# Pooled attention and a multiplicative feed-forward block in one kernel: when the loads start, when the transposes start, and what GpSimd waits for between them

## The chip, the cores and the metric

One core of one Trainium2 chip. The metric is device time in microseconds (us), lowest is best. Each run is labelled fast or slow. On one core there is no second die to compare, so "slow" here only says that a run took over 1.5% more than the fastest run of the same kernel; comparisons and ratios below use fast runs, and where only slow runs show something, the text says so.

TensorE (PE) does matrix products, VectorE (DVE) and ScalarE (ACT) work element by element, GpSimd (POOL) here only issues loads, and SyncE (SP) issues the DMA transposes and the stores. In the profile, L133 is line 133 of the kernel that was run; the changed kernel's lines are numbered a little differently.

## The reference

Attention over 8 batches, 8 heads, 1152 keys of 64 dimensions, with queries averaged in pairs (576 of them), then a feed-forward block with a product of two branches and no nonlinearity:

```python
q_pool = q.reshape(B, H, S // 2, 2, D).mean(axis=3)
scores = (q_pool @ k.transpose(0, 1, 3, 2)) / sqrt(D)
attn   = softmax(scores)
x      = heads_to_columns(attn @ v)             # 4608 x 512
out    = ((x @ w1) * (x @ w2)) @ w3 @ w_out     # 4608 x 512
```

## The kernel before

Two heads are worked on together; such a **pair** has the number P, from 0 to 31. Keys and queries have to be transposed before the scores. For pairs 0 to 8 TensorE transposes them; from pair 9 (`NPE`) on, DMA does it. Per pair there are three loads (k, q, v, from float32 to float16), a copy `kc` that reorders the keys, the pooling of q, a copy of v, and two DMA transposes:

```python
def load(P):                # a "trio": GpSimd issues k, q and v
    load_k(P); load_q(P); load_v(P)        # kst, vst: 4 buffers; qst: 3, each for two pairs

def new_kq(P):
    kT[P] = ab.tile([128, NJ, 128], FP16, tag="kT", bufs=3, name="kT")
    qT[P] = ab.tile([128, NJ, 64], FP16, tag="qT", bufs=3, name="qT")

def prep_dma(P):
    pp, o = P // 2, 64 * (P % 2)
    new_kq(P)
    kc = ab.tile([128, NJ, 2, D], FP16, tag="kc", bufs=2, name="kc")
    nc.vector.tensor_copy(out=kc.rearrange("p j u d -> p u j d"), in_=kst.pop(P))
    nc.sync.dma_start_transpose(out=kT[P], in_=kc.rearrange("p j u d -> p (j u d)"))
    pool_q(P)
    nc.sync.dma_start_transpose(
        out=qT[P], in_=qps[pp][o:o + 64].rearrange("p c u d -> p (c u d)"))
    copy_v(P)
```

The main loop works in iterations of three 512-wide chunks of scores (`BURST = 3`); `at` is the position of the scores, counted in pairs. Between the scores it puts value matmuls (`pv`) by a fixed plan, and pieces of the feed-forward block:

```python
for it in range(NIT):
    at = it * BURST * CH / PAIR             # 1536 / 5184 = 0.296 pairs an iteration
    for w in range(BURST):
        scores(BURST * it + w)              # TensorE: psc = kT, qT
        expo(BURST * it + w)                # ScalarE: er = exp(psc)
    ...                                     # [cut] pairs below NPE
    while staged >= NPE and loaded < NP and at >= loaded - (5.0 if loaded == 9 else 3.4):
        load(loaded)
        loaded += 1
    ...
    elif prepped < NP and at >= prepped - 1.75:
        prep_dma(prepped)
        prepped += 1
    ...                                     # [cut] value matmuls and feed-forward pieces
```

An output row block is copied by VectorE into `osb` (3 buffers) and stored by SyncE, in the same queue as the transposes:

```python
osbs[i] = ffp.tile([128, dm], FP32, tag="osb", bufs=3, name="osb")
...
nc.vector.tensor_scalar_mul(out=osb, in0=p[:, 0:n], scalar1=1.0 / (SCL * SCL))
...
eng.dma_start(out=dst[f // 64][:, cs], in_=osbs[i][64 * z:64 * z + 64, cs])     # nc.sync
```

The softmax here doesn't subtract the row's maximum and nothing guards it: scores larger than these inputs give would overflow.

## Time and profile before

| | before |
|---|---|
| time, median of the first 3 runs (range) | 457.09 us (451.55 to 460.79) |
| profiled run: time, span | 449.39 us, 447.6 us |
| TensorE busy | 410.6 us, 92% of the span |
| ScalarE, VectorE, GpSimd busy | 73%, 48%, 17% |
| landing of kT, qT (min / median / max) | 3.4 / 7.0 / 22.3 us, 2.8 / 9.4 / 21.5 us |

The page is read from its slices (where is TensorE not full?) to the waits (on what?) to the chain that ended last (is that wait on the path?) to the timelines of single engines. "Landing" is the time from the issue of a DMA until its data are there. The prediction below shows the lines.

### The profile page before, as it was taken

The numbers are of one execution on the slowest core, as the hardware profiler recorded it, in microseconds if no ns is written. First come the engines' busy times: TensorE is split into PE (matmuls) and PEld (weight loads), VectorE is DVE, ScalarE is ACT, GpSimd is POOL, SyncE is SP. The second block draws the span as 40 slices with busy tenths as digits, with TensorE's granted clock in tenths as the row PEclk, the third lists the DMA queues.
The fourth block names the chain that finished last, engine by engine and source line by source line (L and its number), as shares of the span: only waits on it lengthen the run. The fifth ranks groups of instructions, "written<-read, shape, count | busy, mean of one in ns | idle before, by whom it ended". The sixth has DMA issues, their size and how long they took to land.

```text
span 447.6 us, 12693 instructions
## 1 busy us (share of the span) xinstructions
PE 410.6 (92%) x5450; PEld 271.2 (61%) x5450; DVE 214.5 (48%) x445; ACT 327.0 (73%) x356; POOL 74.6 (17%) x113
## 2 busy tenths in 40 slices
PE   3989999991999999974799999999999999999996
PEld 1667787761477567742477567765775686544443
DVE  2556555661454655551354564565555644623130
ACT  4898899882688889873488889889788889323332
POOL 8424233230121121210032021230100000000000
PEclk9999999997899999998799999999999999999999
DMA  8999999999599999999599999999992262031304
GB/s 133 207 208 201 178 199 169 192 186 134 65 159 184 151 140 154 123 135 126 75 162 190 143 135 156 146 178 117 157 171 42 55 103 62 15 72 36 80 16 94
DMA packets 94216, 58.71 MB, mean 131 GB/s; under 512 B 64848, under 2 KB 84560, under 8 KB 94160
## 3 DMA queue, kind: packets, MB, share of 16 engines
q0 software_dynamic: 26544, 33.56, 50.4%
q1 hardware_dynamic: 67456, 24.22, 41.5%
q8 instruction: 42, 0.69, 0.7%
q10 hardware_dynamic: 160, 0.13, 0.1%
q14 instruction: 14, 0.11, 0.1%
HBM read 67.11 MB, written 9.44 MB: 171 GB/s over the span
## 4 chain that ended last, share of the span: by engine, by line
PE 77%; DMA 14%; ACT 6%; issue 1%; DVE 0%; POOL 0%; SPq 0%; ACTq 0%; DVEq 0%; POOLq 0%
PE psc L239 16%; PE po L263 16%; PE pp L374 14%; PE pa L356 13%; PE pb L356 13%; DMA qT<-qp 12%; ACT er L249 6%; PE pT L340 3%; DMA kst<-in_k_dram 1%; PE w3t L328 1%; DMA out_dram<-osb 1%; PE t L153 1%; PE tk L153 0%; POOL qst L79 0%; ACT osb L383 0%
## 5 line engine op out<-in xcount | busy, mean ns | idle before, releaser
L249 ACT ACTIVATE er<-psc 128x1024 f16<-128x1024 f32 x324 | 307.8, 1026 | 69.5 <-PE psc L239 69.2
L263 PEld LDWEIGHTS <-er 128*128 128x128 f16 x2880 | 104.7, 98 | 27.0 <-issue 9.7
L239 PE MATMUL psc<-qT,kT 64*128 64x512 f16 (+7 forms) x1152 | 98.9, 293 | 22.9 <-DMA qT<-qp 17.8
L263 PE MATMUL po<-vt,er 128*128 128x65 f16 x2880 | 112.2, 194 | 3.8 <-issue 3.1
L368 DVE TENSOR_TENSOR gT<-pb,asb 128x512 f16<-128x512 f32 x72 | 49.7, 690 | 63.0 <-PE pb L356 62.4
L239 PEld LDWEIGHTS <-kT 64*128 64x128 f16 x1152 | 46.8, 95 | 48.7 <-issue 17.6
L356 PE MATMUL pb<-xT,w2sb 128*128 128x512 f16 x288 | 75.5, 385 | 0.0
L356 PE MATMUL pa<-xT,w1sb 128*128 128x512 f16 x288 | 75.4, 385 | 0.0
L374 PE MATMUL pp<-T,gT 128*128 128x256 f16 (+1 forms) x488 | 67.9, 292 | 0.0
L366 DVE COPY asb<-pa 128x512 f32<-128x512 f32 x55 | 38.0, 691 | 47.6 <-PE pa L356 46.5
L87 POOL DMA_DIRECT2D kst<-in_k_dram x33 | 24.3, 738 | 201.5 <-DVE kc L132 178.6
L374 PEld LDWEIGHTS <-gT 128*128 128x128 f16 x488 | 45.9, 98 | 19.3 <-issue 3.7
L356 PEld LDWEIGHTS <-w2sb 128*128 128x128 f16 x288 | 26.7, 99 | 33.9 <-issue 6.2
L356 PEld LDWEIGHTS <-w1sb 128*128 128x128 f16 x288 | 25.3, 99 | 30.8 <-issue 7.8
L386 DVE TENSOR_SCALAR osb<-pp 128x256 f32<-128x256 f32 x49 | 20.8, 424 | 41.3 <-PE pp L374 32.9
L280 DVE TENSOR_TENSOR xn<-po,rz 128x320 f16<-128x320 f32 x64 | 31.5, 492 | 2.2
L276 DVE RECIPROCAL rz<-po 128x5 f32<-128x5 f32 x64 | 12.3, 193 | 39.5 <-PE po L263 38.7
L364 ACT COPY asb<-pa 128x512 f32<-128x512 f32 x17 | 9.9, 585 | 26.3 <-PE pa L356 26.3
L94 POOL DMA_DIRECT2D vst<-in_v_dram x32 | 23.4, 732 | 16.7 <-DMA kst<-in_k_dram 6.7
L79 POOL DMA_DIRECT2D qst<-in_q_dram x32 | 19.7, 615 | 10.8 <-DMA vst<-in_v_dram 2.7
L383 ACT ACTIVATE osb<-pp 128x512 f32<-128x512 f32 (+1 forms) x12 | 7.0, 579 | 15.5 <-PE pp L374 14.3
L125 DVE COPY vt<-vst 128x1152 f16<-128x1152 f16 x32 | 16.7, 522 | 0.6 <-DMA vst<-in_v_dram 0.5
(37 smaller groups left out, 123.6 us busy)
## 6 DMA issues: line engine op xcount, KB each, us to landing
qst<-in_q_dram POOLq DMA_DIRECT2D x32, 288.0 KB, 11.3
vst<-in_v_dram POOLq DMA_DIRECT2D x32, 288.0 KB, 12.5
out_dram<-osb SPq DMA_DIRECT2D x70, 128.0 KB, 3.5
kst<-in_k_dram POOLq DMA_DIRECT2D x31, 288.0 KB, 10.2
w3h<-in_moe_w_dram POOLq DMA_DIRECT2D x4, 512.0 KB, 15.0
xT<-in_moe_w_out_dram POOLq DMA_DIRECT2D x2, 512.0 KB, 14.1
xT<-xn SPq DMA_TRANSPOSE x64, 6.3
w1sb<-in_moe_w_dram POOLq DMA_DIRECT2D x2, 512.0 KB, 16.4
```

The lines of the kernel that those rows point to most:

```text
L79: nc.gpsimd.dma_start(out=qst[P // 2][o:o + 64].rearrange("p u t d -> p u (t d)"), in_=q[b, h0:h0 + 2].rearrange("u (p t) d -> p u (t d)", ...
L87: nc.gpsimd.dma_start(out=kst[P][:, :, js[0]:js[1], :], in_=k[b, h0:h0 + 2].rearrange("u (p j) d -> p u j d", j=NJ)[:, :, js[0]:js[1], :])
L94: nc.gpsimd.dma_start(out=vst[P].rearrange("p u j d -> p u (j d)"), in_=v[b, h0:h0 + 2].rearrange("u (p j) d -> p u (j d)", j=NJ))
L239: nc.tensor.matmul(t[:, u, o:o + ln], kT[P][s, j, :], qv[s, f0:f0 + ln], start=True, stop=True)
L249: nc.scalar.activation(out=er[:, :, r:r + CH], in_=psc.pop(c), func=AF.Exp, bias=0.0, scale=SCALE)
L263: nc.tensor.matmul(po[P, u][:, VW * i:VW * i + D + 1], er[:, u, r:r + 128], vts[P % 4][:, u, j, 0:D + 1], start=(m == 0), stop=(m == 44), ...
L280: nc.vector.tensor_tensor(out=xn[:, :, u, :], in0=acc[:, :, 0:D], in1=rz.to_broadcast([128, 5, D]), op=ALU.mult)
L356: nc.tensor.matmul(p, w[:, mc, ft * 128:ft * 128 + 128], xT[:, mc, t0:t0 + 512], start=(mc == 0), stop=(mc == NC - 1))
L366: nc.vector.tensor_copy(out=asb[ft], in_=p)
L368: nc.vector.tensor_mul(out=gT[:, ft, :], in0=p, in1=asb.pop(ft))
L374: nc.tensor.matmul(p[:, 0:n], gT[:, ft, 128 * i:128 * i + 128], T16[:, ft, n * s:n * s + n], start=(ft == 0), stop=(ft == NF - 1))
L386: nc.vector.tensor_scalar_mul(out=osb, in0=p[:, 0:n], scalar1=1.0 / (SCL * SCL))
```

## The change

The stated intent: bursts of three chunks, loads timed by the position of the attention, and a GpSimd copy of transposed tiles ahead of each load. The core of the diff:

```diff
+    seen = const.tile([1, 2], FP16)
-            qst[P // 2] = stage.tile([128, 2, 18, D], FP16, tag="qst", bufs=3, name="qst")
+            qst[P // 2] = stage.tile([128, 2, 18, D], FP16, tag="qst", bufs=2, name="qst")
 [in pool_q: one add of 64 partitions for each pair, where before it was one of 128 for two pairs]
-        kT[P] = ab.tile([128, NJ, 128], FP16, tag="kT", bufs=3, name="kT")
-        qT[P] = ab.tile([128, NJ, 64], FP16, tag="qT", bufs=3, name="qT")
+        kT[P] = ab.tile([128, NJ, 128], FP16, tag="kT", bufs=4, name="kT")
+        qT[P] = ab.tile([128, NJ, 64], FP16, tag="qT", bufs=4, name="qT")
 [end of prep_dma]
-        copy_v(P)
+    def settled(P):
+        nc.gpsimd.tensor_copy(out=seen[:, 0:1], in_=kT[P][0:1, 0, 0:1])
+        nc.gpsimd.tensor_copy(out=seen[:, 1:2], in_=qT[P][0:1, 0, 0:1])
 [main loop; after the staging of an early pair, load(loaded) now only if staged <= 4]
-        while staged >= NPE and loaded < NP and at >= loaded - (5.0 if loaded == 9 else 3.4):
+        while 8 <= loaded < 11 and at >= loaded - 3.4:
             load(loaded)
             loaded += 1
-        elif prepped < NP and at >= prepped - 1.75:
+        elif prepped < NP and at >= prepped - 2.2:
             prep_dma(prepped)
+            if 11 <= loaded < NP:
+                settled(prepped)
+                load(loaded)
+                loaded += 1
             prepped += 1
+        if NPE <= copied < NP and at >= copied - 1.2:
+            copy_v(copied)
+            copied += 1
```

`settled` is called the **gate** below, and the 1.75 or 2.2 pairs between the transposes and their use the **lead**.

More of the change, by code (lines that the diff above doesn't have):

```diff
@@ L108, in pool_q @@
             qps[pp] = ab.tile([128, NJ, 2, D], FP16, tag="qp", bufs=2, name="qp")
-        if P < NPE or P % 2 and P == NPE:
-            r = slice(o, o + 64)
-        elif P % 2 == 0:
-            r = slice(0, 128)
-        else:
-            return
+        r = slice(o, o + 64)
         src = qst[pp][r].rearrange("p u (c two) d -> p u c two d", two=2)
@@ L428 @@
     load_w3(2)
-    loaded, staged, prepped = 4, 1, 1
+    loaded, staged, prepped, copied = 4, 1, 1, NPE
     rest = prep_first()
@@ L511 @@
             staged += 1
-            load(loaded)
-            loaded += 1
+            if staged <= 4:
+                load(loaded)
+                loaded += 1
             if staged <= 3:
                 load_ffn(staged - 2)
-        while staged >= NPE and loaded < NP and at >= loaded - (5.0 if loaded == 9 else 3.4):
+        while 8 <= loaded < 11 and at >= loaded - 3.4:
             load(loaded)
@@ L524 @@
                 urgent = True
-        elif prepped < NP and at >= prepped - 1.75:
+        elif prepped < NP and at >= prepped - 2.2:
             prep_dma(prepped)
+            if 11 <= loaded < NP:
+                settled(prepped)
+                load(loaded)
+                loaded += 1
             prepped += 1
+        if NPE <= copied < NP and at >= copied - 1.2:
+            copy_v(copied)
+            copied += 1
         n = PVS[it]
```

## The prediction

> **What bounds the kernel now.** I read the 40 slices of the page first, to see where TensorE (PE) is not full; then the list of waits, then the chain that ended last, then the timelines around the holes.
>
> The slices (11.2 us each; PE, granted clock, DMA engines):
>
> ```profile
> PE   3989999991999999974799999999999999999996
> ...
> PEclk9999999997899999998799999999999999999999
> DMA  8999999999599999999599999999992262031304
> ```
>
> PE is at 8 or 9 tenths nearly everywhere after the first slice: where it is fed, the kernel is bound by TensorE. There are two holes, the 1 of the tenth slice (101 to 112 us) and the 7, 4, 7 further on (190 to 224 us), and the clock falls in the same places. The DMA row is full until about 330 us. The waits (who waited for what: us in total, times, longest):
>
> ```profile
> POOL kst L87 <- DVE kc L132: 178.6, 18, 24.1
> ...
> PE psc L239 <- DMA qT<-qp: 17.8, 3, 9.8
> ...
> PEld L239 <- DMA kT<-kc: 11.2, 2, 7.3
> ...
> PE po L263 <- issue: 3.1, 1, 3.1
> ```
>
> The only large waits of PE after the start are for the DMA transposes kT and qT of a pair of heads; PEld's 11.2 us lie inside the same holes, so they are not added. The pool line is the other half of the story: GpSimd issues the loads, and it issues each as soon as the copy kc (VectorE, L132) frees a slot. The chain that ended last (start us, us, what):
>
> ```profile
> 91.07 21.27 DMA qT<-qp
> 112.38 0.98 PE psc L239 x6
> 113.36 1.82 PE pa L356 x4
> ...
> 193.28 21.55 DMA qT<-qp
> ...
> 303.49 12.53 DMA qT<-qp
> ```
>
> Three transposes are on the path. They belong to pairs 9, 17 and 25: the plan of value matmuls repeats every 27 iterations of three chunks, which is 8 pairs. The timeline of the first hole on VectorE, GpSimd, SyncE's queue, then PE:
>
> ```profile
> 89.11 0.45 DVE L132 COPY kc<-kst 128x1152 f16<-128x1152 f16 x1
> ```
> ```profile
> 89.86 0.72 POOL L87 DMA_DIRECT2D kst<-in_k_dram  x1 [2.62 <-DVE kc L132]
> ...
> 97.33 0.71 POOL L87 DMA_DIRECT2D kst<-in_k_dram  x1 [5.23 <-DVE kc L132]
> ```
> ```profile
> 89.71 1.26 SPq L133 DMA_TRANSPOSE kT<-kc  x1
> 91.07 5.61 SPq L135 DMA_TRANSPOSE qT<-qp  x1
> ```
> ```profile
> 112.38 0.98 PE L239 MATMUL psc<-qT,kT 64*128 64x448 f16 x6 [9.85 <-DMA qT<-qp]
> 113.30 1.89 PE L356 MATMUL pa<-xT,w1sb 128*128 128x512 f16 x4
> ```
>
> The copy kc releases two things at once: the transposes of that pair (89.71, 91.07) and, 0.15 us after the first, a new trio of loads (k, q, v). So every transpose starts against a fresh load. I asked for the time to landing of kT and qT pair by pair: with loads beside them 5.7 to 22.3 us (16.6 and 21.3 for pair 9, 22.3 and 21.5 for pair 17); after the last load, past 332 us, 3.4 to 3.9 us and 2.8 to 4.6 us. Contention costs a transpose a factor of two to six.
>
> **What the Trainium skill says.** "DMA: Bandwidth & Descriptors", Queues, rings and completion order: each DMA engine goes round the queue rows that have work, a whole packet at a time. By the page's queue table GpSimd's loads average 33.56 MB / 26544 = 1264 B a packet, SyncE's queue (transposes and stores) 24.22 MB / 67456 = 359 B; equal turns then favour the loads, which agrees with the landings above. Same page, Anatomy of one DMA: DMA engines do not wait on semaphores, the wait is made by the issuing sequencer. The GpSimd line agrees: the load sat in GpSimd behind kc. So the Python place of a load (the "at" condition) delays nothing by itself; only something GpSimd must wait for does. "TensorE: Matmul & The Clock Gate", Part 1: after an idle window the array runs at half clock until it has been busy some us. It agrees: four pa matmuls took 1.89 us at 113.30, and 1.04 us when warm.
>
> **The change, part by part.**
> 1. Burst: already 3 chunks before; PE's and ScalarE's instruction order is the same in both kernels (10,902 PE rows in each). Worth 0.
> 2. Transposes of pairs 9 to 31 are issued at P-2.2 instead of P-1.75. An iteration is 1536/5184 = 0.296 pairs, so 0.45 pairs is 1 or 2 iterations of about 3.2 us: 3 to 6 us more lead (two iterations for pair 9). kT and qT get 4 buffers for 3, so that this makes no wait.
> 3. The gate: from load 11 on, GpSimd copies one element of kT and of qT of pair P, and only then issues load P+2. It adds 42 tiny GpSimd copies (21 pairs), which wait for both landings; GpSimd has 17% busy. The loads move from about 4 pairs ahead (slots freed by kc of P-4) to 2.2 pairs ahead less the landing. The transposes then meet only the tail of the previous trio, stores, and the xT transposes.
> 4. pool_q goes back to one 64-row add per pair: order shows 31 for 20, at 0.75 us each, so 11 x 0.75 = 8.3 us of VectorE, which is 48% busy: beside PE. qst goes from 3 to 2 buffers, which holds the early loads back a little. copy_v moves to P-1.2, so VectorE does not block on v, which lands last; free.
>
> What leaves the path: idle of PE in the three holes, from its timeline: 9.85 (pair 9) + 3.11 (the "issue" gap at 198.6, where nothing that the profile shows is waited for, in the middle of the DMA jam) + 7.59 (pair 17) + 0.33 + 0.18 (pair 25) = 21.1 us. Then cold matmuls, against the same groups warm: after the first hole 0.37 (psc) + 0.85 (first pa) + 0.43 (pb) = 1.65; after 201.69 us 0.5 + 0.63 + 0.1 = 1.2; after 214.87 us 0.37 + 0.85 + 0.4 = 1.6. Sum 4.5 us. Together 25.6 us. I take them from the run that was profiled, 449.39 us, because only its holes are known: 449.4 - 25.6 = 423.8 us. For leftovers in the dense stretches I add 2 us: **426 us**. The timed runs of before spread from 451.55 to 460.79, which I read as holes of differing size; if so, they shrink too.
>
> **Does the rest still fit?** Landing alone, kT then qT need about 1.3 + 4 = 5 to 6 us; then GpSimd issues three loads in 2 us, and k, q, v landed 6.3, 7.8, 9.4 us after issue at 121 us. Load P+2 therefore has k at about 5.5 + 6.5 = 12 us and q at 15 us after prep P, and is needed two pairs later, about 22 us at the stall-free 11.4 us a pair ((206.9 - 3.1 - 112.4) / 8). Estimate of DMA work per pair: 0.89 MB of loads at the 208 GB/s of the load-heavy 12 to 30 us, 4.3 us; 0.59 MB of transposes at 54 GB/s / 0.32 share = 169 GB/s (332 to 345 us), 3.5 us; 0.29 MB of stores at 53 / 0.24 = 220 GB/s, 1.3 us: 9.1 of 11.4 us. It fits, but not by much in the dense stretches, where prep runs every 9.7 us (187.87 to 197.57).
>
> **Rivals.**
> A. *The DMA queue is the bound, and ordering only moves the wait.* For it: the DMA row is full, and in the dense stretches 9.1 stands against 9.7 us. Then loads land late, VectorE blocks on kc (a wait "DVE kc <- DMA kst"), and PE with it. Against it: no kc after the first pair waited for kst before, and 22 us of lead against 12 to 15. It would give 435 to 450 us.
> B. *Another transfer becomes the victim*: the gate keeps loads off kT and qT but not off the xT transposes, or off whatever the 3.11 us "issue" gap waits for. No xT wait is on the list of before. It would leave some 5 us: about 431.
> C. *The transfers were hidden in most runs and only earlier issue matters*: then the gate is needless, but the time is the same, 424 to 428.
> D. *GpSimd or VectorE becomes the bound*: 42 tiny copies and 8 us cannot do it from 17% and 48%.
>
> **Range and chances.** The middle is the sum above. Below: the timed runs cannot go far under span without holes, so 418. Above: rival B or part of A, 439. The 2% line is 457.09 x 0.98 = 448, reached only if A holds in full. Faster 0.93, same 0.05, slower 0.02.
>
> **What would show it.** The hole digits of PE gone, the clock at 9 throughout from slice 1; "PE psc <- DMA qT" under 3 us in total; no DMA qT piece over 8 us on the chain; landings of kT and qT at medians of 4 to 7 us, not 7.0 and 9.4; GpSimd's large wait turned from kc to DMA kT or qT; loads issued a few us after the transposes, never together with them; span near 424. If holes remain with short landings, my cause is wrong; if VectorE waits for kst, rival A is right.

## The result, and the profile after

| | before | changed |
|---|---|---|
| median (range), 4 runs each | 454.32 us (451.55 to 460.79) | 432.88 us (428.98 to 435.35) |
| ratio of fast runs | | 0.954, 95% interval 0.941 to 0.967 |
| profiled span | 447.6 us | 429.4 us |
| TensorE busy | 410.6 us, 92% | 407.0 us, 95% |
| VectorE busy | 214.5 us | 221.5 us |
| landing of kT (min / median / max) | 3.4 / 7.0 / 22.3 us | 3.4 / 6.5 / 11.0 us |
| landing of qT | 2.8 / 9.4 / 21.5 us | 2.9 / 6.8 / 11.0 us |
| landing of v (median) | 12.5 us | 9.1 us |

Ratios are the mean time of one kernel's fast runs over that of the other's of the same rounds, so not quite the ratio of the medians. A second set of runs of the unaltered changed kernel, on another chip, gave 431.65 us and 0.957 (0.950 to 0.963), with 7.5 us of PE waits for output buffers in its trace:

> The changed kernel unaltered, so that the others of this call have it on the same chip. 429 to 436 us, ratio to before 0.94 to 0.965; VectorE waits 8 to 15 us in all for output buffers, PE holes of 2 to 6 us where it does; no PE wait for kT or qT over 1 us.

The slices of the changed kernel (10.7 us each; TensorE, granted clock, DMA engines):

```profile
PE   3899999999999999899999996999999999999996
...
PEclk9999999999999999999999998999999999999999
DMA  8999999949999999997899979999999531040404
```

The holes of before (digits 1 and 7, 4, 7) are gone. What is left is a 6 at about 257 to 268 us and an 8 at about 172 us. The DMA row is nearly as full as before (packets take 89.3% of the engines' time after 92.6%, for the same bytes): the same work, in another order. The waits (us in total, times, longest), longest first:

```profile
POOL seen L135 <- DMA kT<-kc: 159.0, 20, 16.4
...
POOL seen L136 <- DMA qT<-qp: 32.6, 18, 7.1
...
DVE osb L385 <- DMA out_dram<-osb: 13.7, 5, 6.2
...
PE psc L238 <- DVE osb L385: 4.8, 2, 3.2
```

GpSimd's long wait has moved from the copy kc to the landed transposes, and no wait of TensorE for kT or qT is on the list. A new one is: TensorE waits 4.8 us for VectorE's output copy, and that one waits for stores to give a buffer back. How the gate works shows in the timeline, first SyncE's queue and then GpSimd, for pair 9, the simplest case (start us, duration us):

```profile
90.93 1.27 SPq L129 DMA_TRANSPOSE kT<-kc  x1
92.30 1.26 SPq L131 DMA_TRANSPOSE qT<-qp  x1
```

```profile
94.36 0.18 POOL L135 COPY seen<-kT 1x1 f16<-1x1 f16 x1 [16.38 <-DMA kT<-kc]
95.23 0.71 POOL L136 COPY seen<-qT 1x1 f16<-1x1 f16 x1 [0.69 <-DMA qT<-qp]
95.88 0.71 POOL L88 DMA_DIRECT2D kst<-in_k_dram  x1
```

Both transposes were down about 3 us after their issue, and only then did the next trio start. Most pairs are not so lucky: the trio that one pair's gate sets free runs into the transposes of the next pair. Pair 16:

```profile
160.93 1.26 SPq L129 DMA_TRANSPOSE kT<-kc  x1
```

```profile
161.54 0.73 POOL L88 DMA_DIRECT2D kst<-in_k_dram  x1 [1.67 <-issue]
```

Its transposes were down 12.4 us after the issue of kT. In this trace 21 of the 23 pairs meet loads between the issue of kT and the landing of qT, and in 11 of them a load is issued in that time. What is gone are the cases with further trios on top. Counted over the profiled runs of all 14 kernels (slow runs and the wrong result of early_only included), by the loads (k, q, v each one) that are under way when kT is issued or start within 4 us after it, the time from the issue of kT to the landing of qT was:

| loads met | pairs | time | over 14 us |
|---|---|---|---|
| none | 34 | 4.0 to 5.9 us | 0 |
| 1 to 3 | 212 | 4.9 to 23.4 us | 3 |
| 4 or 5 | 65 | 6.1 to 30.5 us | 21 |
| 6 or more | 11 | 10.8 to 27.0 us | 8 |

In the six kernels whose gate waits for kT and qT no pair met more than 5 and none took over 13.4 us; in the kernel before, pair 9 met 9 and took 22.6 us. The table goes by count alone and is no experiment: no run limits the number of loads without also ordering them.

The 3.25 us hole that is left, on TensorE, then VectorE, then SyncE's queue:

```profile
264.18 0.61 PE L238 MATMUL psc<-qT,kT 64*128 64x512 f16 x2 [3.25 <-DVE osb L385]
264.72 1.89 PE L373 MATMUL pp<-T,gT 128*128 128x256 f16 x8
```

```profile
263.70 0.42 DVE L385 TENSOR_SCALAR osb<-pp 128x256 f32<-128x256 f32 x1 [4.30 <-DMA out_dram<-osb]
```

```profile
251.29 2.33 SPq L129 DMA_TRANSPOSE kT<-kc  x1
253.73 1.86 SPq L131 DMA_TRANSPOSE qT<-qp  x1
255.69 4.86 SPq L394 DMA_DIRECT2D out_dram<-osb  x6
```

Six half-block stores stand behind two transposes, in one queue and beside a trio issued at 250.51 us. Three output buffers hold three row blocks; the fourth copy waits 4.30 us, the PSUM tile (the buffer of TensorE's results) that it should empty stays taken, and TensorE stops. In the chain that ended last the DMA pieces of kT and qT are gone, and these stand in their place:

```profile
164.34 9.79 DMA out_dram<-osb
...
256.29 7.29 DMA out_dram<-osb
```

**The account of the difference.** The spans differ by 447.6 - 429.4 = 18.2 us. The prediction took 25.6 us of holes off the path. The trace of the changed kernel has these of its own: 1.54 us (at 173.5 us) and 3.25 us (at 260.9 us) for an output buffer, 1.5 us of cold matmuls (those that run slower just after a hole) after the second (on the chain, pp 1.82 for 0.98 us and pa 1.38 for 0.97 us; psc 0.61 for 0.39 us), and 1.26 us at 74.5 us, where VectorE waited for early loads of q and v. 25.6 - 1.54 - 3.25 - 1.5 - 1.26 = 18.05 us, which is the 18.2 us within 0.2 us.

### The profile page after: what moved, and what is told of

The parts are those of the page before. It is cut to its first block, busy times and chain, and to the rows that moved or that the text cites. A ratio compares the mean times of both kernels' runs of the same rounds, so it can differ in the third digit from the quotient of the medians.

```text
span 429.4 us, 12797 instructions
## 1 busy us (share of the span) xinstructions
PE 407.0 (95%) x5450; PEld 269.5 (63%) x5450; DVE 221.5 (52%) x456; ACT 327.0 (76%) x356; POOL 83.7 (20%) x155
## 4 chain that ended last, share of the span: by engine, by line
PE 81%; DMA 9%; ACT 5%; DVE 2%; issue 1%; SPq 1%; POOL 0%; DVEq 0%; ACTq 0%; POOLq 0%
PE po L262 18%; PE psc L238 17%; PE pa L355 15%; PE pb L355 15%; PE pp L373 12%; ACT er L248 5%; DMA out_dram<-osb 5%; DMA vst<-in_v_dram 4%; PE pT L339 2%; DMA kst<-in_k_dram 1%; PE t L152 0%; DVE osb L385 0%; PE w3t L327 0%; SPq L131 0%; SPq L394 0%
## 5 line engine op out<-in xcount | busy, mean ns | idle before, releaser
L238 PE MATMUL psc<-qT,kT 64*128 64x512 f16 (+7 forms) x1152 | 97.8, 290 | 11.5 <-DVE osb L385 4.8
L355 PE MATMUL pb<-xT,w2sb 128*128 128x512 f16 x288 | 74.1, 380 | 0.0
L373 PE MATMUL pp<-T,gT 128*128 128x256 f16 (+1 forms) x488 | 68.8, 295 | 0.0
L135 POOL COPY seen<-kT 1x1 f16<-1x1 f16 x21 | 4.6, 217 | 159.0 <-DMA kT<-kc 159.0
L275 DVE RECIPROCAL rz<-po 128x5 f32<-128x5 f32 x64 | 12.4, 193 | 38.6 <-PE po L262 37.8
L112 DVE TENSOR_TENSOR qp<-qst 64x1152 f16<-64x1152 f16 x31 | 23.2, 750 | 5.6 <-DMA qst<-in_q_dram 5.1
L80 POOL DMA_DIRECT2D qst<-in_q_dram x32 | 19.7, 616 | 10.2 <-DMA w2sb<-in_moe_w_dram 2.5
```

Of the source, the lines that this page charges most:

```text
L112: nc.vector.tensor_tensor(out=qps[pp][r].rearrange("p c u d -> p u c d"), in0=src[:, :, :, 0, :], in1=src[:, :, :, 1, :], op=ALU.add)
L238: nc.tensor.matmul(t[:, u, o:o + ln], kT[P][s, j, :], qv[s, f0:f0 + ln], start=True, stop=True)
L355: nc.tensor.matmul(p, w[:, mc, ft * 128:ft * 128 + 128], xT[:, mc, t0:t0 + 512], start=(mc == 0), stop=(mc == NC - 1))
L373: nc.tensor.matmul(p[:, 0:n], gT[:, ft, 128 * i:128 * i + 128], T16[:, ft, n * s:n * s + n], start=(ft == 0), stop=(ft == NF - 1))
```

## The experiments

Two questions are open after the traces. Is it the gate or the lead that took the holes away, and within the gate, is it that loads start after the transposes, or that fewer trios are under way? And is the store wait really what is left? Each call of runs has its own runs of the kernel before on the same chip; their medians were 453.28, 451.41 and 452.68 us.

### The lead alone: early_only

```diff
 kernel before
-  kT, qT: bufs=3            at >= prepped - 1.75
+  kT, qT: bufs=4            at >= prepped - 2.2
```

> The kernel before with the earlier transposes alone: lead 2.2 pairs instead of 1.75 and 4 buffers for kT and qT, no gate, loads as before. Theory G (the gate does it, because a load beside them slows the transposes): landings of kT and qT stay as in before, medians 7 to 10 us and longest over 15 us; the lead of 3 to 6 us takes a part of each hole, PE waits for DMA qT or kT of 3 to 12 us in total remain, time 437 to 448 us, ratio to before 0.965 to 0.985. Theory L (the lead does it, the gate is needless): no PE wait for kT or qT over 1 us, time 429 to 435 us, ratio about 0.95.

Measured: 445.76 us (445.48 to 446.07), ratio 0.986 (0.982 to 0.990). The result is **wrong** (relative error 0.288). I worked out why from the plan of value matmuls: with the copy of v still in `prep_dma`, a lead of 2.2 puts it, for 6 of the 23 pairs (9, 14, 17, 22, 25, 30), ahead of the last value matmuls of the pair four earlier, whose slot it overwrites; with 1.75 that happens for none. So moving `copy_v` to P - 1.2 is what makes the earlier transposes legal. I take the times as those of this instruction order, with all instructions in place; no run tests whether the wrong values change them, and 2.3 us of TensorE's waits here, which no other run has, are for that copy of v, so the lead alone may be worth up to that much more. The waits and the chain:

```profile
PE psc L239 <- DMA qT<-qp: 8.5, 1, 8.5
PE psc L239 <- DVE osb L386: 6.2, 3, 2.9
```

```profile
91.09 19.98 DMA qT<-qp
```

Landings stayed at up to 16.8 (kT) and 20.0 us (qT). The lead of one or two iterations hid the later holes but not the one of pair 9. This is what the theory of the gate expected; 1.4% is about a third of the change's 4.6%. TensorE's wait for output buffers (`osb`), which the kernel before did not have, is there too, without any gate.

### The gate with the old lead: gate_late

```diff
 changed kernel
-        elif prepped < NP and at >= prepped - 2.2:
+        elif prepped < NP and at >= prepped - 1.75:
```

> The changed kernel with the lead put back from 2.2 to 1.75 pairs; the gate stays. Theory G: landings 3.4 to 11 us as in the changed kernel, no PE wait for kT or qT over 2 us, time 430 to 435 us, ratio about 0.95. Theory L: the holes at pairs 9, 17 and 25 come back with 10 us or more of PE idle, time 442 to 455 us.

Measured: 426.96 us median; the fast runs 424.20, 427.88 and 426.03 us, one slow run of 438.75 us; ratio 0.942 (0.934 to 0.950). No PE wait for kT or qT; landings up to 11.8 us. So the gate does not need the longer lead, and the fast runs were if anything shorter than the changed kernel's. A likely reason shows in SyncE's queue of the profiled run, in the stretch where the changed kernel has its first store hole:

```profile
161.91 4.54 SPq L394 DMA_DIRECT2D out_dram<-osb  x4
166.62 1.32 SPq L129 DMA_TRANSPOSE kT<-kc  x1
168.04 1.33 SPq L131 DMA_TRANSPOSE qT<-qp  x1
```

With the lead at 1.75 four stores go ahead of the transposes; with 2.2 the transposes (160.93 and 162.31 us) and a trio (161.54 us) go first and six stores follow. The wait of VectorE for output buffers was 6.2 us here, all in the tail. With 3 output buffers every profiled kernel with the lead of 2.2 has TensorE waiting for them, with the gate (4.8 and 7.5 us, gate_kc 7.4 us) or without (6.2 us in early_only, 15.9 and 16.9 us below), and neither kernel with 1.75 has, with the gate or without: the store holes go with the lead. The slow run was not profiled, so what made it long is open.

### No gate: no_gate and no_gate_q3

```diff
 changed kernel
             prep_dma(prepped)
             if 11 <= loaded < NP:
-                settled(prepped)
                 load(loaded)
 [no_gate_q3 also: qst bufs=2 -> 3]
```

> The changed kernel without the two one-element copies on GpSimd; everything else stays, also the 2 buffers of q. Theory G: loads start again at once with kc, and since q has only 2 buffers they start two trios at a time; landings of kT and qT rise to medians of 8 to 12 us, some over 18 us, holes return, time 438 to 455 us. Theory L: 429 to 435 us and no PE wait for kT or qT.

> The changed kernel without the gate and with 3 buffers of q as before, so that loads start one trio at a time with each kc, as in the kernel before; lead 2.2 and the later copy of v stay, so the result is right. Theory G: as the run with the earlier transposes alone, 440 to 450 us, landings up to 15 to 22 us, PE waits for qT or kT of 3 to 12 us. Theory L (lead alone): 424 to 434 us.

Measured: no_gate 459.24 us median, fast runs 457.21 and 450.58 us, ratio 1.004 (0.985 to 1.023). no_gate_q3 466.11 us, fast runs 464.41 to 466.60 us, ratio 1.031 (1.025 to 1.036). Without the gate, everything else of the change together gains nothing. The waits of no_gate (its profile fell on a slow run) and then of no_gate_q3 (a fast one):

```profile
PE psc L238 <- DMA qT<-qp: 19.2, 4, 10.7
PE psc L238 <- DVE osb L385: 16.9, 3, 14.3
```

```profile
PE psc L238 <- DVE osb L385: 15.9, 3, 11.1
PE psc L238 <- DMA qT<-qp: 12.8, 3, 6.6
```

Both kinds of hole are there, and landings reach 21.6 and 22.2 us in no_gate_q3. My expectation for no_gate_q3, 440 to 450 us as early_only, missed: it is some 20 us slower. Its loads of v wait for the later copy of v (GpSimd 197.0 us), so v of one pair and k and q of the next start together, often with the transposes; whether that is the whole reason no run tells.

### The gate on the transposes' source: gate_kc

```diff
 changed kernel, in settled
-        nc.gpsimd.tensor_copy(out=seen[:, 0:1], in_=kT[P][0:1, 0, 0:1])
-        nc.gpsimd.tensor_copy(out=seen[:, 1:2], in_=qT[P][0:1, 0, 0:1])
+        nc.gpsimd.tensor_copy(out=seen[:, 0:1], in_=kc_of[P][0:1, 0, 0, 0:1])
+        nc.gpsimd.tensor_copy(out=seen[:, 1:2], in_=kc_of[P][0:1, 0, 1, 0:1])
```

Loads stay one trio per pair and two pairs ahead, but each starts with the transposes.

> The changed kernel with the two GpSimd copies reading kc (the transposes' source) in place of kT and qT (their result): loads stay two pairs ahead and one trio per pair, with the same count of GpSimd instructions, but each trio starts together with the transposes and not after them. Theory G (a load beside a transpose is what is slow): landings of kT and qT back to medians of 8 to 12 us, longest over 14 us; PE waits for them 2 to 15 us in all; 436 to 448 us. Theory N (it is the number of trios in flight: one trio per pair, two pairs ahead, is enough): landings under 11 us, no such PE wait, 425 to 434 us as the changed kernel.

Measured: 432.49, 456.83, 446.27 and 439.28 us, of which only the first is fast. Its trace has landings of 8.9 (kT) and 8.6 us (qT) at the median and 15.4 and 12.8 us at most, against 6.1 and 6.9, and 12.9 and 12.0 us in the run of the changed kernel on the same chip, but no PE wait for them; its holes are stores (7.4 us). So this run did not tell the two theories apart, and it was made again below without the store holes. Nor does this gate hold down what a pair meets: between the issue of kT and the landing of qT up to 9 loads were under way in this trace, against 5 in the changed kernel's, so it doesn't separate the order from the number either.

### More output buffers: osb6, before_osb6

```diff
-                    osbs[i] = ffp.tile([128, dm], FP32, tag="osb", bufs=3, name="osb")
+                    osbs[i] = ffp.tile([128, dm], FP32, tag="osb", bufs=6, name="osb")
```

> The changed kernel with 6 output buffers (osb) for 3. Theory S (what is left of the holes is VectorE waiting for an output buffer that a slow store holds, and TensorE behind it): the wait DVE osb for DMA out_dram falls from 13.7 us to under 4 us before the tail, the 1.54 and 3.25 us holes of PE go, with some 1.4 us of cold matmuls, so 5 to 6 us less than the changed kernel: 425 to 428 us, ratio to before about 0.94. Theory Q (the DMA queue as a whole is the bound, the store wait is only where it shows): the wait moves to kst, qst or xT and the time stays at 430 to 434 us.

> The changed kernel with 6 output buffers once more, as the reference for this call: 423 to 426 us in every run, spread under 2 us, ratio to before about 0.94.

> Control: the kernel before with 6 output buffers. Its trace had no PE wait for an output buffer outside the tail, so the holes of kT and qT stay as they are: ratio to before 0.99 to 1.0, PE waits of 10 to 20 us for qT. If stores were the common cause, it would gain 4 us or more.

Measured: the changed kernel with 6 buffers 424.51 us (423.47 to 424.81), ratio 0.938 (0.933 to 0.944), and again on another chip 424.27 us (423.18 to 425.66), ratio 0.938 (0.934 to 0.941): all eight runs within 2.5 us (under 2 us was expected of the second set, which has the whole 2.5). The kernel before with 6 buffers: 453.45 us, ratio 1.001 (0.997 to 1.006). The slices of osb6_again, and its waits of PE after the first pair:

```profile
PE   3898999999999999999999999999999999999996
```

```profile
PE psc L238 <- ACT er L248: 4.3, 11, 0.7
```

Its span is 421.2 us; VectorE's wait for stores is one of 6.2 us, in the tail. The first set, at 424.51 us, came out a little under the 425 to 428 us expected. What was left in the changed kernel was therefore mostly the stores, and the DMA engines as a whole do not bound it. In the kernel before, the same buffers give nothing: TensorE still waits 17.5 us there for qT. The store hole is a wait that the change brought in, with the lead of 2.2, not an old one.

### Output buffers crossed with the gate: gate_kc_osb6 and no_gate_osb6

```diff
 gate_kc and no_gate, each with
-  tag="osb", bufs=3
+  tag="osb", bufs=6
```

> The gate on kc with 6 output buffers: each trio starts together with the transposes, one trio per pair, and stores can no longer hold VectorE. Theory O (the order counts: transposes must be down before the loads start): PE waits for kT or qT in some runs, 428 to 445 us, spread over 5 us. Theory N (one trio per pair, two pairs ahead, is enough; the scatter of 432 to 457 us of the run with 3 output buffers was stores): 423 to 427 us in every run, as the reference of this call.

> The changed kernel without the gate, with 6 output buffers. Theory G: the store holes go (16.9 us of PE in the run with 3 buffers), the holes of kT and qT stay (19.2 us there): 436 to 448 us. Rival S2 (without the gate, too, stores are the larger part and transposes follow from them): under 432 us.

Measured: gate_kc_osb6 451.77, 436.37, 436.82 and 425.48 us (only the last fast); no_gate_osb6 438.66, 446.46, 462.45 and 462.30 us (only the first fast). The trace of gate_kc_osb6 fell on the 451.77 us run. GpSimd, SyncE's queue and TensorE in its first hole:

```profile
95.70 0.72 POOL L88 DMA_DIRECT2D kst<-in_k_dram  x1
...
104.33 0.72 POOL L88 DMA_DIRECT2D kst<-in_k_dram  x1
```

```profile
96.96 3.01 SPq L130 DMA_TRANSPOSE kT<-kc  x1
100.06 8.09 SPq L132 DMA_TRANSPOSE qT<-qp  x1
```

```profile
124.85 0.50 PE L239 MATMUL psc<-qT,kT 64*128 64x384 f16 x2 [11.52 <-DMA qT<-qp]
```

A trio started 1.26 us ahead of kT, the next one before qT was down, qT landed after 24.75 us, and TensorE stood for 11.52 us. In this run TensorE waited 22.6 us in all for qT. Its slices:

```profile
PE   3879999999089999984799999999999999999996
...
PEclk9999999999679999999699999999999999999999
```

The granted clock is at 9 in every slice except beside the holes, so the lower mean clock of this "slow" run comes from the holes. The one fast run of this kernel (425.48 us) is as good as any with the gate on the landing. What the runs show is a matter of scatter: with the gate on the landing and 6 buffers, 8 of 8 runs lie between 423.2 and 425.7 us; with the gate on kc and 6 buffers, 1 of 4, so theory N (423 to 427 us in every run) did not hold. That it is the order, and not the number of loads met (8 for the pair shown), is not shown: this run has both. no_gate_osb6 has 9.5 us of PE waits for qT in its one fast run, with kT landings of up to 26.9 us, and no store wait outside the tail: the gate is needed with 6 output buffers as with 3.

### The best candidate: late_osb6_q3

```diff
 changed kernel
-  at >= prepped - 2.2      osb bufs=3    qst bufs=2
+  at >= prepped - 1.75     osb bufs=6    qst bufs=3
```

> The changed kernel with the lead put back to 1.75 pairs, 6 output buffers and 3 buffers of q. Theory: the gate does all, the lead nothing; the output buffers take the store holes; 3 q buffers give back the 1.3 us that the first 90 us lost. 421 to 425 us in every run, spread under 2 us, ratio to before about 0.935; no PE wait over 1 us between 20 us and the tail. Rival: with less lead some pair is late in some runs, spread over 4 us or median over 427 us.

Measured: 426.11, 423.30 and 424.08 us fast, one slow run of 431.13 us; ratio 0.941 (0.936 to 0.946). The expectation missed in part: the slow run lies outside 421 to 425 us and the fast ones spread over 2.8 us, and the trace of the 426.11 us run has PE waits of 1.6 and 0.8 us near 178 us, where VectorE waited 0.82 us for a load of k and 1.12 us for one of q. It does not beat the changed kernel with 6 output buffers alone, which is the best version found: 424.3 to 424.5 us, some 1.8% under the changed kernel. Both kernels with the old lead had one longer run in four (438.75 and 431.13 us), and the eight runs with the lead of 2.2 and 6 buffers had none. Whether the lead buys that steadiness is open; four runs each are too few. The third q buffer has no effect that these runs show; the first feed-forward matmul, which marks the end of the early phase, started at 81.8 us with it and at 81.3 to 82.8 us in the five profiled runs with the gate on kT and qT and two q buffers.

## Why the prediction was right, and where it was off

- **The time.** 426 us was forecast, in a range of 418 to 439; 432.88 us was measured. The direction and the range held, and so did the main part of the mechanism: the holes for kT and qT went, and it was the gate that took them. How the gate does it was wrong in part (see part 3).
- **What leaves the path (25.6 us).** Confirmed. The forecast of a run without holes was a span of 447.6 - 25.6 = 422.0 us; osb6_again, the run without holes, has 421.2 us, and its runs a median of 424.27 us against the 423.8 us of the sum.
- **The step that was mis-sized** is "For leftovers in the dense stretches I add 2 us". It was 7.55 us in the profiled run: 4.79 us of idle and 1.5 us of cold matmuls from stores, and 1.26 us in the early phase. I looked for the victim among the inputs of the scores and of the feed-forward block. The outputs share SyncE's queue with the transposes, and I did not ask how many stores would stand behind an earlier pair of transposes. The early 1.26 us did not recur at that size in gate_late or osb6, and before_osb6, which has none of the change, has one of 1.3 us, so it need not come from the change.
- **Rival B** ("Another transfer becomes the victim", about 431 us) is what happened, in form and in size; the victim was the store, which it did not name. For "whatever the 3.11 us 'issue' gap waits for" the packed trace has a candidate: TensorE went on 1.53 us after a 16 KB packet of the instruction queue had ended, and gaps of this kind in before_osb6, no_gate_q3 and osb6 (3.37, 3.15 and 0.58 us) ended 1.58, 1.39 and 1.35 us after such a packet. So the transfer that was late there may have been one of instructions; no run tests it.
- **Rival A** (the DMA queue is the bound) fell: the DMA row is nearly as full as before, and yet with six output buffers TensorE is busy 96% of the span and waits for no transfer after the first pair. The estimate of 9.1 of 11.4 us of DMA work per pair was good enough.
- **Rival C** (the gate is needless) fell: without it the other parts gave 1.004 and 1.031 times the time of before.
- **Part 2, the lead**, was described rightly as one or two iterations more, but alone it is worth 1.4%, and it is what sets transposes and a trio ahead of the stores. I had not asked what it does to them.
- **Part 3, the gate.** Its counts held. "The transposes then meet only the tail of the previous trio" and the sign "never together with them" did not: in the changed kernel's trace 21 of 23 pairs met loads, and for pair 27 the trio started 0.05 us after kT. By the traces, what the gate takes away are the further trios on top of one; no run tests that apart from the order.
- **Two readings of before that were off.** "So every transpose starts against a fresh load" holds for 16 of 23 pairs (a load issued between kT's issue and qT's landing), and most of these made no hole; pairs 9 and 17 met 12 and 6 loads in that time, but so did pair 24 (6), without a hole. The third transpose on the chain (303.49 us) is pair 26's and not pair 25's, so the plan's repeat every 8 pairs does not explain it; the prediction lays 0.5 us of its 25.6 to it. That equal turns favour the loads' larger packets was not tested by any run.
- **Part 4**: VectorE gained 7.0 us of work (8.3 forecast), beside TensorE. "copy_v moves to P-1.2 ... free" missed its real purpose: without it the earlier preparation overwrites v that is still in use.
- **What would show it.** Held: holes gone, no wait for qT or kT on TensorE's list, no qT piece on the chain, landings of 6.5 and 6.8 us, GpSimd's wait turned to kT and qT, each gated trio within about 2 us of the landing. Not held: loads never together with the transposes (part 3); the clock has one 8, after the store hole, and the span is 429.4 us and not near 424.

## What to carry to other kernels

A DMA issue waits only for what its queue's engine must wait for; its place in the program delays nothing (before, GpSimd waited 178.6 us in all for kc, whatever the load's `at` condition). So if two streams disturb each other, make the issuing engine read one element of what must be down first. Such a gate need not clear the way to help: here most transposes still shared the DMA engines with one trio of loads, and what went were the cases with more. When a wait is removed, look at everything in the same queue, stores above all, and count the buffers that hold it up: here six output buffers instead of three turned 429 to 435 us into a steady 424.

## What the Trainium skill lacked or had wrong

- "DMA: Bandwidth & Descriptors", Rules for kernel authors: it says that a transpose next to ordinary DMAs needs nothing. That holds for the result in all correct runs here, but not for time: a kT transpose that lands in 3.4 to 3.9 us without loads took up to 22.3 us beside them in the kernel before and 26.9 us in no_gate_osb6. The page has no figure for this.
- The same page, Anatomy of one DMA: its fit for a load from GpSimd, 2.0 us plus bytes over 436e3, makes an estimate of 2.7 us for 288 KB (294,912 bytes written). The medians here are 10.2 to 12.5 us before and 5.8 to 9.1 us with the gate; even the 96 KB piece of the first k load, with a load of q issued before it, took 3.8 us, where the fit makes an estimate of 2.2 us. The page gives no fit for loads in company.
- No page that I read has a one-element GpSimd copy as a means to hold loads back until transposes have landed and so shorten them, or says what it costs: 0.18 us at the median, 42 of them here, off the path.
- "TensorE: Matmul & The Clock Gate", Part 1, was right here: at the end of the holes of 3.11 us (before) and 3.25 us (changed kernel) the granted clock falls to half for 3.41 us, and on the chain eight pp matmuls take 1.82 us that take 0.98 us when warm; after the hole of 1.54 us it stays full.
